# From the second pair of units on: three one-pass products of split operands in place of f32 products with Strassen

## The chip, the core and the metric

One NeuronCore of a Trainium2 chip. The metric is the device time of one execution, in microseconds (us), lower is better. Engine names: PE is TensorE, DVE is VectorE, ACT is ScalarE, POOL is GpSimd, SP is SyncE (it issues most DMAs).

## The reference

A Mamba-2 scan (4 batches, 8 heads, 768 tokens, 32 channels a head, state of 16) in chunks, then a feed-forward block with silu over 3072 tokens (256 to 2048 to 256). All in float32, but the two weight matrices come as float64.

```python
la = log(clip(a, 1e-6, 1)); cum = cumsum(la)          # per chunk
L = exp(cum[:, None] - cum[None, :]) * causal
y = ((C @ B.T) * L) @ x + (C @ state) * exp(cum)
state = exp(sum(la)) * state + (B * exp(cum[-1] - cum)).T @ x
x2 = y.transpose(0, 2, 1, 3).reshape(3072, 256)
h = x2 @ w_in
out = (h / (1 + exp(-h))) @ w_out
```

## The kernel before

**Units.** The 3072 tokens are 12 units of 256; two units make a pair (6 pairs), and three units a batch, whose state goes from unit to unit. For each unit the scan makes decays, a small score matrix and the state, and its result XM (256 channels by 256 tokens). Stage one multiplies XM by w_in and applies silu (result in gT); stage two multiplies by w_out; the result is transposed and stored.

**The scan of a unit.** `load_pa` and `load_ab` bring the decays `a`, spread over partitions by the DMA; f_P (L284 to L291) and f_E (L319 to L336) clamp them on VectorE and make prefix products with a scan instruction (L304 is E's). f_B (L341, POOL) makes BT from E; f_T (L347) or f_TP transposes B and C; f_T2 (L367) and f_C (L373) scale them; f_D0 (L391) and f_G0 (L406) are PE products into the PSUM tile gy; f_M (L417) multiplies the scores by E on VectorE; f_S (L432) carries the state, f_SM (L440) spreads it on ScalarE; f_Y (L460 and L469) makes y in gy, and f_X (L482) evacuates it to XM.

**Weights.** A weight piece (16 of them, `W`) is loaded raw as float64 words (L156). ScalarE (`w_size`, L164 and L168), VectorE (`w_bits`, L176 to L180) and POOL (L184) make f32 from it. Seven raw buffers; w_bits(n) issues the load of piece n+7.

**Stage one.** For units 0 to 3, f_s1 (L505): f32 products of 128x256, silu at L507. From pair 2 on, f_x1 does the two units of a pair with Strassen's seven products in place of eight (L703), with sums on VectorE (L706), copies and silu on ScalarE (L717, L709), and sums of weights and inputs made ahead (f_SW L675, f_XT L686).

**Stage two.** s2_pair, also with seven products in place of eight (L611 and L648, in the one-bank tile o_ps). Its operand sums are made by VectorE (f_T1 L544) and by accumulating DMAs of POOL (f_TS L553); partial results are copied by ScalarE (L588) and added by POOL (L558); f_out (L564, L566) transposes on VectorE and stores by SP. Stage two of a pair is laid piece by piece (`f_s2(n)`) between the products of the next pair's stage one.

**Order.** The instructions of each engine stand in the order in which the program text issues them (`manual_schedule`): the list `steps`, the loops over `j` and `scan_plan`. Each engine works in order, and waits are placed where tiles are shared. PSUM's eight banks are four of gy (one tile, `ps_s`), three of hp and one of o_ps.

**The start.** SP issues, in this order: a for the first batch (L192), C of unit 0 (L115), a again (L200), x of unit 0 (L122), three weight pieces (L156), B, C (L107) and x (L122) of unit 1, and more weight pieces. PE, while it waits, runs `busy` fillers (L226, L228). The decays of units 0 and 1 come by a small product (f_Ab, L312), those of later units by load_ab.

Of the kernel before, what the change touches and what calls it, by code (L numbers as in the profile page):

```python
# [9 lines left out]
U32 = mybir.dt.uint32  # L10
BF16 = mybir.dt.bfloat16
AF = mybir.ActivationFunctionType
# [9 lines left out]
def kernel(  # L22
# [36 lines left out]
    loads = ctx.enter_context(tc.tile_pool(name="loads", bufs=3))  # L59
    loads2 = ctx.enter_context(tc.tile_pool(name="loads2", bufs=2))  # L60
    rawp = ctx.enter_context(tc.tile_pool(name="rawp", bufs=7))
    wtp = ctx.enter_context(tc.tile_pool(name="wtp", bufs=3))
    sc = ctx.enter_context(tc.tile_pool(name="sc", bufs=1))
    sc2 = ctx.enter_context(tc.tile_pool(name="sc2", bufs=2))
    xmp = ctx.enter_context(tc.tile_pool(name="xmp", bufs=4))
    gpool = ctx.enter_context(tc.tile_pool(name="gpool", bufs=4))
    tpool = ctx.enter_context(tc.tile_pool(name="tpool", bufs=1))
    ppool = ctx.enter_context(tc.tile_pool(name="ppool", bufs=5))
    opool = ctx.enter_context(tc.tile_pool(name="opool", bufs=2))
# [5 lines left out]


    pa, ab, bn, tbc, xt = ({} for _ in range(5))
# [4 lines left out]
    def load_pa(u, q):  # L82

        b, t0 = at(u)
        pa[u] = loads.tile([128, UT], FP32, name="pa")
        q.dma_start(out=pa[u], in_=bass.AP(tensor=a.tensor, offset=a.offset + b * H * S + t0,
                                           ap=[[S, H], [0, N], [1, UT]]))

    def load_ab(u, q):

        b, t0 = at(u)
        ab[u] = loads2.tile([128, 2, H, Q], FP32, name="ab")
        for t in range(4):
            k, c = divmod(t, 2)
            q.dma_start(out=ab[u][64 * c:64 * c + 64, k],
                        in_=bass.AP(tensor=a.tensor, offset=a.offset + b * H * S + t0 + t * Q,
                                    ap=[[0, 64], [S, H], [1, Q]]))

    def load_n(u, i, q):

        b, t0 = at(u)
        if i == 0:
            t = bn[u] = loads.tile([128, 2, H, N], FP32, name="bn")
        else:
            t = tbc[u] = loads.tile([128, 2, 2, 8, N], FP32, name="tbc")[:, 0]
        for k in range(2):
            q.dma_start(out=t[:, k], in_=(B, C)[i][b, :, t0 + 128 * k:t0 + 128 * k + 128].rearrange("h p n -> p h n"))  # L107

    def load_t(u, i, q):

        b, t0 = at(u)
        if u not in tbc:
            tbc[u] = loads.tile([128, 2, 2, 8, N], FP32, name="tbc")
        for g in range(4):
            q.dma_start(out=tbc[u][32 * g:32 * g + 32, i],  # L115
                        in_=(B, C)[i][b, 2 * g:2 * g + 2, t0:t0 + UT].rearrange("e (t r) n -> t e r n", r=8))

    def load_x(u, q):
        b, t0 = at(u)
        xt[u] = loads.tile([128, 2, H, D], FP32, name="xt")  # L120
        for k in range(2):
            q.dma_start(out=xt[u][:, k], in_=x[b, :, t0 + 128 * k:t0 + 128 * k + 128].rearrange("h p d -> p h d"))  # L122

    def load_unit(u):
        load_pa(u, nc.sync)
        if 0 < u < UPB:
            load_n(u, 1, nc.sync)
        else:
            load_t(u, 0, nc.sync)
            load_t(u, 1, nc.sync)  # L130
        load_n(u, 0, nc.sync)
        load_ab(u, nc.sync)
        load_x(u, nc.sync)

    w_in_sb = const.tile([128, KC, d_ff], FP32, name="w_in_sb")
    w_out_sb = const.tile([128, NF, d_model], FP32, name="w_out_sb")
# [5 lines left out]
    raw, wu, wv = {}, {}, {}  # L142

    def w_piece(n):
        which, j = W[n]
        if which == "i":
            return wi[:, :, j * WF:(j + 1) * WF], w_in_sb[:, :, j * WF:(j + 1) * WF]
        return wo[:, 2 * j:2 * j + 2], w_out_sb[:, 2 * j:2 * j + 2]

    def load_w(n, q):  # L150
        src, dst = w_piece(n)
        if src.dtype == FP32:
            q.dma_start(out=dst, in_=src)
            return
# [3 lines left out]


    def w_size(n, what="uv"):  # L160
        if n in raw:
            if "u" in what:
                u = wu[n] = wtp.tile([128, 2, WF], FP32, name="wu")
                nc.scalar.activation(u, raw[n][:, :, :, 1].bitcast(FP32), AF.Abs)  # L164
            if "v" in what:
                v = wv[n] = wtp.tile([128, 2, WF], FP32, name="wv")

                nc.scalar.activation(v, raw[n][:, :, :, 0], AF.Copy, scale=2.0 ** -51, bias=2.0)  # L168

    def w_bits(n, parts=1):  # L170
        dst = w_piece(n)[1]
        if n in raw:
            u, v, hi = wu.pop(n), wv.pop(n).bitcast(U32), raw[n][:, :, :, 1]


# [3 lines left out]

# [7 lines left out]


    A0, A1 = 96, 96 + S // Q
    early = gpool.tile([128, NF, UT], FP32, name="gT")  # L190
    ach = early[:, 0:2].rearrange("p a (h t) -> p (a h) t", t=Q)
    nc.sync.dma_start(out=ach[A0:A1], in_=bass.AP(tensor=a.tensor, offset=a.offset, ap=[[Q, S // Q], [S, H], [1, Q]]))  # L192

    flat = early.rearrange("p f t -> p (f t)")
    QZ = 8 * (Q + 1)
    pa01 = flat[:, 6 * UT:8 * UT]
    pz01, one01, pfx01 = (flat[:, 8 * UT + QZ * i:8 * UT + QZ * (i + 1)] for i in range(3))
# [8 lines left out]
    load_x(1, nc.sync)  # L206

    mark = const.tile([1, RAW - 5], U32, name="mark")
    for n in range(3, RAW):
        if n > 4:  # L210
            nc.sync.dma_start(out=mark[:, n - 5:n - 4], in_=raw[n - 2][0:1, 0, 0, 0:1])
        load_w(n, nc.sync)


    def f_A():
        nc.vector.tensor_scalar(out=ach[A0:A1], in0=ach[A0:A1], scalar1=1.0, scalar2=1e-6, op0=ALU.min, op1=ALU.max)
        nc.vector.memset(ach[A0:A1, :, 0:1], 0.0)


    idle = early[:, 4].bitcast(BF16)  # L220
    nc.vector.memset(idle, 0.0)

    def busy(n, small=0):
# [3 lines left out]
        for i in range(small):  # L227
            nc.tensor.matmul(out=t[:64, :64], lhsT=idle[:, 0:64], rhs=idle[:, 64:128], start=True, stop=True)  # L228

    nc.vector.memset(ach[0:A0], 0.0)  # L230

    sel = early[:, 2:4].rearrange("p a (s c t) -> p (a s) c t", s=2, c=2)
    nc.gpsimd.memset(sel, 0.0)
    nc.gpsimd.affine_select(out=sel, in_=sel, pattern=[[-2, 4], [-1, 2], [0, 64]], compare_op=ALU.not_equal,
                            fill=1.0, base=-A0, channel_multiplier=1)

    diag1 = early[:, 5:6, 0:Q]
# [15 lines left out]

# [11 lines left out]

    pz = const.tile([128, 4, Q + 1], FP32, name="pz")
    one = const.tile([128, 4, Q + 1], FP32, name="one")
    for t, n in ((pz, 0.0), (one, 1.0)):
        nc.gpsimd.memset(t, 0.0)
        if n:  # L270
            nc.gpsimd.memset(t[:, :, 0:1], n)
    E, M, BT, BH, CT, CE, CW, PFX, ST, SM, DP, XM, GTS, BX = ({} for _ in range(14))
# [3 lines left out]

# [7 lines left out]
    def f_P0(u):  # L284
        nc.vector.tensor_scalar(out=pz[:, :, 1:], in0=pa.pop(u).rearrange("p (c t) -> p c t", t=Q),
                                scalar1=1.0, scalar2=1e-6, op0=ALU.min, op1=ALU.max)

    def f_P1(u):

        PFX[u] = sc2.tile([128, 4, Q + 1], FP32, name="pfx")  # L290
        nc.vector.tensor_tensor_scan(out=PFX[u].rearrange("p c t -> p (c t)"),  # L291
                                     data0=pz.rearrange("p c t -> p (c t)"),
# [3 lines left out]
    def f_P(u):  # L296
        f_P0(u)
        f_P1(u)

    def scan_E(u, g0, n, t):  # L300

        if g0 == 0:
            E[u] = sc.tile([128, 2, H, Q], FP32, name="E")
        nc.vector.tensor_tensor_scan(out=E[u].rearrange("p k h t -> p (k h t)")[:, Q * g0:Q * (g0 + n)],  # L304
                                     data0=t.rearrange("p g t -> p (g t)"),
                                     data1=diag[:, 0:n].rearrange("p g t -> p (g t)"),
                                     initial=0.0, op0=ALU.mult, op1=ALU.add)

    def f_Ab(u, k):

        ab[u, k] = t = ps_h.tile([128, H, Q], FP32, name="hp")
        nc.tensor.matmul(out=t.rearrange("p h t -> p (h t)"),  # L312
                         lhsT=sel[:A1, 2 * u + k].rearrange("r c m -> r (c m)"),
                         rhs=ach[:A1].rearrange("r h t -> r (h t)"), start=True, stop=True)

    def f_Ek(u, k):
        scan_E(u, H * k, H, ab.pop((u, k)))

    def f_E0(u, i, n):  # L319

        t = ab[u].rearrange("p k h t -> p (k h) t")[:, 2 * H // n * i:2 * H // n * (i + 1)]
        nc.vector.tensor_scalar(out=t, in0=t, scalar1=1.0, scalar2=1e-6, op0=ALU.min, op1=ALU.max)
        nc.vector.memset(t[:, :, 0:1], 0.0)  # L323

    def f_E1(u, i, n):

        g = 2 * H // n
        t = ab[u].rearrange("p k h t -> p (k h) t")[:, g * i:g * (i + 1)]
        scan_E(u, g * i, g, t)
        if i == n - 1:  # L330
            ab.pop(u)

    def f_E(u):
        f_E0(u, 0, 1)
        f_E1(u, 0, 2)
        f_E1(u, 1, 2)  # L336

    def f_B(u, engine=nc.gpsimd):

        BT[u] = sc.tile([128, 2, H, N], FP32, name="BT")  # L340
        engine.tensor_tensor(out=BT[u], in0=bn[u], in1=E[u][:, :, :, Q - 1:Q].to_broadcast([128, 2, H, N]),  # L341
# [3 lines left out]

# [6 lines left out]

# [10 lines left out]
    def f_T2(u, e):  # L363

        if e == 0:
            CE[u] = sc.tile([128, 2, UT], FP32, name="ce")
        nc.scalar.activation(CE[u][:, e], CT[u], AF.Copy, scale=par[:, e:e + 1])  # L367

    def f_C(u):

# [5 lines left out]
    def f_D0(u, early=False):  # L376

# [3 lines left out]
        n = 3 if last else 4  # L381
# [6 lines left out]
        for t in range(n):  # L388
# [8 lines left out]
    def f_G0(u):  # L397

        bh, ce = BH.pop(u), CE[u]
# [14 lines left out]
    def f_M(u, k):  # L414

        M[u] = m = E[u].rearrange("p k (g e) t -> p k g (e t)", e=2)
        nc.vector.tensor_tensor(out=m[:, k], in0=DP[u][:, :, 128 * k:128 * k + 128], in1=m[:, k], op=ALU.mult)  # L417

    def f_S(u, t0=0, t1=4):

        first, last = u % UPB == 0, u % UPB == UPB - 1
        if first and t0 == 0:
            ST[u] = sc2.tile([128, 4, 64], FP32, name="st")
        if not last and t1 == 4:
# [583 lines left out]
```

## Time and profile before

| what | value |
|---|---|
| median of 3 runs | 350.76 us (350.61 to 354.09) |
| profiled execution: span, first to last instruction | 348.7 us; its own time is not given apart |
| busy, of the span | PE 342.7 us, DVE 204.6, ACT 162.8, POOL 113.0 |
| granted PE clock | 1.00 in every window |
| DVE busy in 50 to 70 us | 19.64 of 20 |
| DMA moved | 42.66 MB, 122 GB/s |

Lines of the profile have the form: source line, engine, operation, output<-inputs, partitions x elements, count | busy us, mean ns of one | idle of the engine just before, and what ended it. PEld is the weight load of PE, which runs beside the products. Timeline lines begin with the start and the length in us; lines of the chain too. An f32 product of 128x128 by 128x256 stands as two records of two passes each. The mean of a product's record includes the flow through the array, so products overlap, and the pace is read from groups of them.

### The profile page before, as it was taken

The page shows a single profiled execution, that of the slowest core. Times are in us where ns is not written, and L with a number is a line of the kernel's source. Part 1 is how long each engine was busy: PE and PEld are TensorE (multiplying, and loading weights), DVE is VectorE, ACT ScalarE, POOL GpSimd, SP SyncE. Part 2 cuts the span into 40 slices and gives each one's busy share as a digit, 9 for nine tenths or more (in the row PEclk, how much of TensorE's full clock was granted, in tenths as well). Part 3 has the DMA queues.
Part 4 walks back from the last instruction along what each step waited for, and adds up shares of the span by engine and source line. Part 5 has one row for each costly group of instructions (what it writes and reads, how often), then busy time and mean ns, then how long its engine had stood idle before and what let it go on. Part 6 is the DMA issues. An engine that isn't in the chain of part 4 may idle for free.

```text
span 348.7 us, 8382 instructions
## 1 busy us (share of the span) xinstructions
PE 342.7 (98%) x3324; PEld 288.5 (83%) x3324; DVE 204.6 (59%) x406; ACT 162.8 (47%) x399; POOL 113.0 (32%) x140
## 2 busy tenths in 40 slices
PE   8999999999999999999999999999999999999996
PEld 3678888888888888888888888888888888888886
DVE  7998799976795664544663563564652241233912
ACT  3578395323323545455645454644545454454010
POOL 4355245444285032244042244042235112041200
DMA  6877997799857598948178965056604237512202
GB/s 130 203 237 174 241 313 126 132 199 218 144 102 126 124 186 149 169 102 138 21 159 163 187 112 90 16 98 125 115 2 75 39 60 144 107 24 53 41 7 46
DMA packets 117056, 42.66 MB, mean 122 GB/s; under 512 B 102424, under 2 KB 108824, under 8 KB 117016
## 3 DMA queue, kind: packets, MB, share of 16 engines
q1 hardware_dynamic: 110472, 25.73, 35.8%
q0 software_dynamic: 4464, 16.25, 25.0%
q8 instruction: 26, 0.43, 0.6%
q10 hardware_dynamic: 2080, 0.13, 0.4%
q14 instruction: 14, 0.11, 0.1%
HBM read 22.70 MB, written 3.15 MB: 74 GB/s over the span
## 4 chain that ended last, share of the span: by engine, by line
PE 96%; DVE 1%; issue 1%; POOL 1%; ACT 0%; DVEq 0%; POOLq 0%
PE o_ps L648 36%; PE hp L703 28%; PE hp L505 16%; PE hp L648 3%; PE gy L469 2%; PE gy L406 2%; PE o_ps L611 2%; PE gy L460 2%; PE gy L391 1%; PE hp L626 1%; PE hp L312 1%; PE o_ps L226 1%; POOL w_in_sb L184 1%; DVE E L417 0%; PE o_ps L228 0%
## 5 line engine op out<-in xcount | busy, mean ns | idle before, releaser
L706 DVE TENSOR_TENSOR gT<-hp,p 128x256 f32<-128x256 f32 x64 | 26.9, 420 | 73.6 <-ACT p L717 37.6
L648 PE MATMUL o_ps<-gT,w_out_sb 128*128 128x256 f32 x240 | 60.4, 379 | 0.0
L709 ACT ACTIVATE gT<-gT 128x256 f32<-128x256 f32 x96 | 39.7, 414 | 43.9 <-DVE gT L706 43.9
L505 PE MATMUL hp<-XM,w_in_sb 128*128 128x256 f32 x256 | 59.3, 381 | 0.9 <-ACT XM L482 0.5
L505 PEld LDWEIGHTS hp<-XM,w_in_sb 128*128 128x128 f32 x256 | 48.0, 190 | 8.7 <-POOL w_in_sb L184 1.4
L703 PE MATMUL hp<-raw 128*128 128x256 f32 x192 | 52.7, 380 | 0.0
L558 POOL TENSOR_TENSOR ps<-ps 128x256 f32<-128x256 f32 x35 | 29.6, 845 | 71.1 <-ACT ps L588 69.8
L648 PEld LDWEIGHTS o_ps<-gT,w_out_sb 128*128 128x128 f32 x240 | 45.4, 190 | 6.3
L553 POOL DMA_DIRECT2D gT<-gT x31 | 27.9, 929 | 65.7 <-DVE TN L544 21.5
L703 PEld LDWEIGHTS hp<-raw 128*128 128x128 f32 x192 | 36.2, 190 | 5.4 <-POOL ps L558 0.6
L717 ACT ACTIVATE p<-hp 128x256 f32<-128x256 f32 x64 | 24.6, 384 | 27.4 <-PE hp L703 25.9
L706 DVE TENSOR_TENSOR gT<-hp,u 128x256 f32<-128x256 f32 x32 | 13.6, 424 | 38.6 <-PE hp L703 38.6
L703 PE MATMUL hp<-XM,w_in_sb 128*128 128x256 f32 x128 | 34.1, 389 | 0.0
L507 ACT ACTIVATE gT<-hp 128x512 f32<-128x512 f32 x32 | 18.9, 595 | 26.4 <-PE hp L505 26.3
L703 PEld LDWEIGHTS hp<-XM,w_in_sb 128*128 128x128 f32 x128 | 23.3, 190 | 4.3 <-issue 1.0
L304 DVE TENSOR_TENSOR_SCAN E<-ab,diag 128x256 f32<-128x256 f32 (+1 forms) x32 | 25.1, 826 | 0.8 <-DVE ab L323 0.5
L341 POOL TENSOR_TENSOR BT<-bn,E 128x256 f32<-128x256 f32 x12 | 9.4, 780 | 47.5 <-DVE E L304 39.4
L648 PE MATMUL o_ps<-gT,wu 128*128 128x256 f32 x88 | 22.4, 380 | 0.0
L648 PE MATMUL o_ps<-gT,wv 128*128 128x256 f32 x88 | 22.2, 380 | 0.0
L648 PE MATMUL o_ps<-gT,raw 128*128 128x256 f32 x80 | 20.5, 380 | 0.0
L588 ACT ACTIVATE ps<-o_ps 128x256 f32<-128x256 f32 x35 | 13.3, 383 | 14.8 <-PE o_ps L648 13.0
L703 PE MATMUL hp<-raw,w_in_sb 128*128 128x256 f32 x64 | 19.1, 380 | 0.0
(126 smaller groups left out, 522.3 us busy)
## 6 DMA issues: line engine op xcount, KB each, us to landing
gT<-gT POOLq DMA_DIRECT2D x31, 512.0 KB, 6.3
ab<-in_a_dram SPq DMA_DIRECT2D x40, 128.0 KB, 3.1
raw<-in_moe_w_in_dram SPq DMA_DIRECT2D x8, 512.0 KB, 5.1
raw<-in_moe_w_out_dram SPq DMA_DIRECT2D x8, 512.0 KB, 6.5
xt<-in_x_dram SPq DMA_DIRECT2D x24, 128.0 KB, 5.1
out_dram<-ot SPq DMA_DIRECT2D x92, 32.0 KB, 2.6
bn<-in_B_dram SPq DMA_DIRECT2D x22, 64.0 KB, 5.3
tbc<-in_C_dram SPq DMA_DIRECT2D x40, 32.0 KB, 3.4
```

The costliest lines, as they stand in the source:

```text
L304: nc.vector.tensor_tensor_scan(out=E[u].rearrange("p k h t -> p (k h t)")[:, Q * g0:Q * (g0 + n)], data0=t.rearrange("p g t -> p (g t)"), ...
L341: engine.tensor_tensor(out=BT[u], in0=bn[u], in1=E[u][:, :, :, Q - 1:Q].to_broadcast([128, 2, H, N]), op=ALU.mult)
L505: nc.tensor.matmul(out=hp[:, i], lhsT=w_in_sb[:, kc, f * 128:(f + 1) * 128], rhs=xm[:, kc], start=(kc == 0), stop=(kc == KC - 1))
L507: nc.scalar.activation(GTS[g][:, :, j], hp, AF.Silu)
L553: nc.gpsimd.dma_start(out=o[:, js], in_=a[:, js], accum_op=ALU.add)
L558: engine.tensor_tensor(out=o, in0=p, in1=q, op=op)
L588: nc.scalar.activation(p[m].rearrange("p (k c t) -> p c k t", c=2, k=2), o.rearrange("p (c k t) -> p c k t", c=2, k=2), AF.Copy)
L648: nc.tensor.matmul(out=o, lhsT=w(j), rhs=g()[:, j], start=(j == 0), stop=(j == last))
L703: nc.tensor.matmul(out=o, lhsT=w, rhs=x_, start=start, stop=True, skip_group_check=True)
L706: nc.vector.tensor_tensor(out=o, in0=p, in1=q, op=ALU.add)
L709: nc.scalar.activation(o, i, AF.Silu)
L717: nc.scalar.activation(o, i, AF.Copy)
```

## The change

From pair 1 on, each operand of the two stages is split into parts that hold 12 bits: a high part h, a remainder l = x - h, and d = (1 + 2^-12) h - x. Three products, h of the one operand with h of the other, l with l and d with d, are made in the type float32r and accumulated in PSUM: a burst with h and l, then a scaling by 1 + 2^-12 on ScalarE, then d. The weights are split in the same way. So there are three products in place of one f32 product; Strassen's sums, both stages', are gone, and so are POOL's accumulating DMAs. Pair 0 stays f32, now without Strassen (f_s1, and f_n2 with products of 512 columns). Line numbers below are those of the changed kernel.

The main pieces of the new order (`...` where code is left out):

```python
def w_high(n):                                     # ACT, L200
    t = WK[n, "h"] = small([128, 2, WF], FR)
    nc.scalar.activation(t, WT[n], AF.Copy, scale=LESS * Z)
def w_rest(n, what="ld"):                          # DVE, L205: "r" in the lists
    ...
def f_XH(u): ...                                   # ACT, L466: h of a unit's y
def f_XL(u): ...                                   # DVE, L472, L473: its l and d
def epoch(G, e, fills=(0, 0)):                     # stage one of four blocks of 128
    t = ps_s.tile([128, 4, 512], FP32, name="gy")
    for p in range(2):
        for i in range(2 * p, 2 * p + 2):
            s1_mm(t[:, i], G, 4 * e + i, "hl", True)           # L553, 16 products in a row
        nc.scalar.activation(t[:, 2 * p:2 * p + 2], t[:, 2 * p:2 * p + 2], AF.Copy, scale=1.0 + Z)
    for p in range(2):
        f_s2(fills[p])                                         # L533, stage two
        for i in range(2 * p, 2 * p + 2):
            s1_mm(t[:, i], G, 4 * e + i, "d", False)
        g = GT[G, 2 * e + p] = large([128, 2, 512])
        nc.scalar.activation(g, t[:, 2 * p:2 * p + 2], AF.Silu, scale=BACK)
def f_h(G, i): ...                                 # ACT, L576, 128x1024
def f_ld(G, i):                                    # DVE, L581 and L582, 128x1024 each
    g, h = GT.pop((G, i)), HT.pop((G, i))
    l, d = large([128, 2, 512], FR), large([128, 2, 512], FR)
    ...
def f_ev(P, what): ...                             # ACT L540, DVE L544: end of a pair's stage two

def step(G, n):                                    # four steps a pair
    u = 2 * G + 2 + n // 2
    ...
    S2.extend(NEXT)
    f_s2(6)
    if prev: f_h(*prev[0])
    if more and n % 2 == 0: f_G(u); f_BX(u); f_M(u)            # in gy
    elif more: f_Y(u); f_YS(u)                                 # in gy
    if prev: f_h(*prev[1])
    f_s2(12)
    if G > 1 and n == 1: f_s2(24); f_ev(G - 1, "ad")
    epoch(G, n, (3, 3))                                        # in gy
    ...
    if G == 1: steps(early[n])                                 # weights: r, h
    if prev: f_ld(*prev[0])
    if more and n % 2 == 0: f_S(u); f_SM(u)
    elif u + 1 < NU and n % 2 == 1 and more: f_E(u + 1); f_B(u + 1)
    if prev: f_ld(*prev[1])
    ...
```

f_ld also puts 12 products of stage two into the list NEXT, which the next step takes up. Where the step ends in `...`, the transposes of unit u + 1, its prefix and cw, XH, XL, the loads and the output of a pair are issued. So gy (four banks) holds in turn a burst of the scan (D0 and G, or Y) and the four blocks of an epoch; accumulators of stage two hold the other four. All 4 KB tiles (`large`: silu results, h, l, d, outputs) come from one pool of 12 buffers taken in turn. After the last pair, 48 products of stage two remain, then f_ev and two f_out.

The decays of units 2 to 11 are now clamped once for all, at the start, on POOL, and go to DRAM (az, ac), from where load_ab and load_pz (eight DMAs a unit) spread them:

```diff
+    for b in range(batch):
+        nc.sync.dma_start(out=araw[CPB * b:CPB * b + CPB], ...)     # after load_x(1)
...
+    nc.gpsimd.memset(acp[:, :, 0:1], 0.0)
+    for t in (azt, acp[:, :, 1:]):
+        nc.gpsimd.tensor_scalar(out=t, in0=araw, scalar1=1.0, scalar2=1e-6, op0=ALU.min, op1=ALU.max)   # L285
+    nc.gpsimd.memset(azt[:, :, 0:1], 0.0)
+    nc.gpsimd.dma_start(out=az, in_=azt.rearrange("p h t -> p (h t)"))
+    nc.gpsimd.dma_start(out=ac, in_=acp.rearrange("p h t -> p (h t)"))
...
-    nc.vector.tensor_scalar(out=t, in0=t, scalar1=1.0, scalar2=1e-6, op0=ALU.min, op1=ALU.max)
-    nc.vector.memset(t[:, :, 0:1], 0.0)
+    nc.vector.tensor_tensor_scan(out=o, data0=src, data1=diag..., initial=0.0, op0=ALU.mult, op1=ALU.add)   # f_E, L319
```

These POOL instructions stand in the program before the first f_B. The order of POOL at the start is then: memsets and selects, L285 twice, a memset, two DMAs, BT of unit 0 (L324), cw (L352), the weight sums (L194). Between f_s1 of pair 0 and pair 1, f_n2 is interleaved with weight pieces 13 to 15, the remainders `r` and the scans of units 3 and 4:

```python
for n, todo in ((2, "b13 s14 2X"), (2, "r0 3T h2"), (2, "b14 s15 3E 3B"), (2, "3P 3C r1 h3"), (2, "b15 3GMS"),
                (2, "4L r2 h4"), (2, "r3 4T"), (2, "3Y h5"), (2, "4E 4B 4P 4C"), (2, "5L 3X h6 h7"), (2, "r4 r5 h8 h9")):
    f_n2(n); steps(todo)
early = {0: "r6 r7 h10 h11", 1: "r8 r9 h12 h13", 2: "r10 r11 h14 h15", 3: "r12 r13 r14 r15"}
```

## The prediction, on record before the run

> **What bounds the kernel now.** First the page: span, busy shares and the chain of work that ended last.
>
> ```profile
> span 348.7 us, 8382 instructions
> ...
> PE 342.7 (98%) x3324; PEld 288.5 (83%) x3324; DVE 204.6 (59%) x406; ACT 162.8 (47%) x399; POOL 113.0 (32%) x140
> ...
> PE 96%; DVE 1%; issue 1%; POOL 1%; ACT 0%; DVEq 0%; POOLq 0%
> ```
>
> TensorE is 98% busy and 96% of the chain: only its own work, or a new wait of it, can move the end. Next, the pace, in the chain told in order of time:
>
> ```profile
> 163.92 2.21 PE hp L703 x10
> ...
> 170.01 1.73 PE hp L703 x8
> ...
> 217.82 2.21 PE hp L703 x10
> ...
> 271.84 2.21 PE hp L703 x10
> ...
> 277.94 1.73 PE hp L703 x8
> ```
>
> Eight records are four f32 products of 256 columns: 1.73/8 = 0.216 us per record of two passes. One of the steady pairs recurs every 53.9 us (163.92, 217.82, 271.84). Then the start, POOL's timeline and SP's queue:
>
> ```profile
> 8.07 0.73 POOL L341 TENSOR_TENSOR BT<-bn,E 128x256 f32<-128x256 f32 x1 [2.75 <-DVE E L304]
> 9.98 0.68 POOL L373 TENSOR_TENSOR cw<-ct,gT 128x256 f32<-128x256 f32 x1 [1.18 <-DVE gT L280]
> 14.11 1.42 POOL L184 TENSOR_TENSOR w_in_sb<-wu,wv 128x256 uint32<-128x256 uint32 x2 [3.44 <-DVE wv L180]
> ```
>
> ```profile
> 9.34 5.18 SPq L107 DMA_DIRECT2D tbc<-in_C_dram  x2
> 14.57 1.31 SPq L122 DMA_DIRECT2D xt<-in_x_dram  x2
> 15.93 1.09 SPq L156 DMA_DIRECT2D raw<-in_moe_w_in_dram  x2
> ```
>
> POOL makes unit 0's BT at 8.07, and everything of the scan hangs on it; SP is still issuing unit 1's x at 15.88. Last, the rows by shape, for prices on VectorE and ScalarE:
>
> ```profile
> L417 DVE TENSOR_TENSOR E<-gy,E 128x512 f32<-128x512 f32 x24 | 15.4, 681 | 0.0
> ...
> L304 DVE TENSOR_TENSOR_SCAN E<-hp,diag 128x512 f32<-128x512 f32 x4 | 4.9, 1221 | 0.2
> ...
> L675 DVE TENSOR_TENSOR raw<-w_in_sb 128x1024 f32<-128x1024 f32 x2 | 2.5, 1270 | 0.0
> ...
> L675 DVE TENSOR_TENSOR raw<-w_in_sb,raw 128x1024 f32<-128x1024 f32 x1 | 1.2, 1218 | 0.0
> ```
>
> Successive VectorE instructions overlap by some 0.08 us (two of L417 take 1.28 together in the timeline), so I charge 0.6 for a two-input 128x512 and 1.15 for a 128x1024.
>
> **TensorE's own work.** From pair 1 on, each pair has 96 + 96 products of 512 columns. If a float32r product is one pass it costs 0.216, as any 512 column-passes do now, with the weight load (190 ns a row) hidden as now: 41.5 us a pair. Scans, by busy time of L469, L406, L460, L391 (10.3+8.3+7.9+5.4)/12 = 2.66 a unit, add 5.3: 46.8 instead of 53.9. No run here shows the dtype. Bounds: 0.216, and twice that if it needs two passes; the first is taken because f32's four passes already run at 512 columns per 0.216. Pair 0 stays f32 and loses Strassen: 32 products of 512 columns, 4x0.216 each, 27.6.
>
> The Trainium skill ("TensorE: Matmul & The Clock Gate", Back-to-back issue gap) puts a sustained stream of 512-column products at about 131 ns each. That would make the 960 products 82 us cheaper than 0.216 does; the rows show no stream that fast.
>
> Without any wait: stage one of pair 0 with unit 2's scan ends at 50.5 (start of L611 in the timeline); then 27.6 for stage two of pair 0, 8.0 for units 3 to 5, 31.1 for pair 1 (144 products): 117.2. Pairs 2, 3, 4: 140.4. Pair 5, with no scan: 41.5. The last 48 products, no longer laid under a later pair: 10.4. Then the end: two ScalarE copies and two VectorE additions 2.0, two 128x512 transposes 1.6 (L564 has 432 ns for half), four DMA issues and a landing of 2.6 (out_dram): 8. Sum 317.5. So the most that the change can gain is 31 us.
>
> **The new wait at the start.** POOL now clamps `araw` (L285, twice) and issues two DMAs (az, ac) ahead of BT of unit 0. The four araw loads stand behind unit 1's x in SP's queue: issue from 15.9 at 0.45 each, and in front of them x, whose median to landing is 5.1. Landing 20.3 (19.0 to 21.5). A POOL tensor_scalar of 512 elements is in no row: between memset 0.53 and the two-input 1.40; I take the one-input select, 0.67. DMA issues on POOL: L553 has 0.93 (0.45 if like SP's). BT starts at 20.3+1.3+0.2+1.9 = 23.7 and ends at 24.45; unit 0's L391 products, at 9.67 now, start at 24.5: +14.8 us (12.2 to 17.8). Behind the waiting POOL stand BT, cw and all weight sums; behind them the state update, M and the weight bits on VectorE, SM and w_size on ScalarE, Y and stage one on TensorE. Nothing covers it: az is wanted only for unit 2.
>
> The granted clock is 1.00 in every window, but the five fillers at 1.26 take 2.31 us, and three at 11.02 take 0.81. The same page (What's actually happening) says that an idle window of about 3.4 us drops the clock to half, and the same length of work raises it again. This idle of 15 us would by that rule cost up to 1.7 us more; I charge none, since VectorE's chain leads there.
>
> **VectorE's backlog before pair 2.** After the bits of weight piece 8 (36.4 now) VectorE still has pieces 9 to 15 at 2.36 each (49.08, 51.45, 53.81 in the timeline), scans of units 2 to 4, and the new remainders `r`, 32 at 0.6. What TensorE waits for, walked in program order: unit 3's E ends 28.5 after 36.4 (six pieces 14.2, two E 4.8, prefix, cw, M, state 3.2, XL, r0, transposes 3.5, hand-overs from ScalarE and TensorE 2.8), plus BT 0.8, so at 80.5 with the shift; TensorE is there at 50.5+14.8+8.6 = 73.9: 6.6. In step (1,1) SM sits on ScalarE behind the two evacuations of pair 0: 3.5; the burst behind ys: 1.2; M of unit 5 behind r8 to r11: 1.6; two SM and one M later: 1.3. Together 14.2 (bounds: 0, if VectorE is never late, and twice).
>
> **The steps of pairs 2 to 4.** Let T be the end of the burst of 16 products. TensorE ends the step at T+3.0 and reaches the next burst at T+8.0 (six products 1.3, D0 and G 1.1, twelve 2.6). In the last step of a pair the second remainder d0 gets its buffer (12 of 4 KB, in turn) only from the last three fills, T+1.75. From there VectorE: d0 1.15, E 2.4, l and d 2.3, prefix 0.7, XL 1.2, transpose 0.8, M 1.2 = 9.75, so M ends at T+11.6. D0 waits for BT 2.0, the burst for M 1.7. In the step after ev, the like chain costs 1.9; odd steps wait 0.6 each for SM, which ScalarE does behind the silu, and 0.3 for the second copy. A full pair: 7.0 of waits (bounds: 0 to 12), the first 3.9, as its d0 was free early: 17.9. ScalarE is loaded 16 of 25 us over two steps (128x1024 at 1.02: 384 for 256, 595 for 512, 211 more per 256). The 5 more loads a unit (22, not 17, by SP at 0.55) lie inside 25 us; were they late, E of a later unit would wait.
>
> What goes away, the accumulating DMAs, Strassen's sums and POOL's L558, lies beside TensorE now: credited at nothing.
>
> **Sum:** 317.5 + 14.8 + 14.2 + 17.9 = 364.4 of span, against 348.7. The median of the runs (350.76) is 2.1 over the profiled span; the profiled execution's own time is not given apart. Forecast 366.5.
>
> **Rivals.**
> Rival A, faster: VectorE keeps ahead. E, M and the remainders are done before TensorE arrives, no step waits: 317.5+14.8+2.1 = 334. For it: VectorE has 18.5 us of work in two steps of 23.4. Against: its order, d0 behind a late buffer and M behind XL. It decides where the chain from d0 to M is under 6.2 us instead of 9.75; already at 7.5, with half of the backlog gone, the time is under 347.
> Rival B, no change: the start is hidden (araw lands early or POOL's part is short), so 14.8 goes: 352. Against: POOL works in order, and SP issued x at 14.57 to 15.88.
> Rival C: further waits, weights and loads that arrive late behind the shift or hand-overs that I set at nothing: 385 and more. For it: my walk charges no semaphore latency.
> Rival D: float32r takes two passes: 960x0.216 = 207 more, about 570. This is the change not doing what it says.
>
> **Numbers.** Forecast 0.62, Rival A (and halfway to it) 0.18, Rival B 0.08, Rival C 0.08, Rival D 0.04. The measurement tells about 1% from no change: 347.3 to 354.3. Faster 0.18, same 0.10 (Rival B and a slice of the forecast's low end), slower 0.72. The range reaches from halfway into A, 343, over the bounds of the start (+3) and of the steps (+12) to 382; the forecast's own is 355 to 380.
>
> **What would show it.** Right: POOL idle to about 20 us, then L285, BT at about 24; TensorE idle from 10 to 24; L553 and L533 at 0.216 start to start; pair period about 54 with TensorE waiting for BT (L324) and M (L400) in even steps; VectorE the releaser in pairs 2 to 4; some 8 us from the last product to the end. Wrong: BT near 8; products at 0.43; a pair period of 47.

## The result, and the profile after

446.88 us median of 4 runs (445.94 to 448.55) against 350.69 for the kernel before: ratio 1.273, 95% interval 1.267 to 1.279. Slower, as forecast, but 80 us above the forecast of 366.5 and 65 above the upper end of its range (382). The profiled execution took 445.94, its span is 444.2.

The page of the changed kernel: span, busy shares, the chain of work that ended last, and the first group of part 5.

```profile
span 444.2 us, 7604 instructions
...
PE 352.3 (79%) x3082; PEld 246.4 (55%) x3082; DVE 250.5 (56%) x338; ACT 197.3 (44%) x293; POOL 50.5 (11%) x62
...
PE 65%; ACT 16%; DVE 8%; issue 4%; SPq 3%; POOL 1%; DMA 0%; DVEq 0%; ACTq 0%; POOLq 0%
...
L553 PE MATMUL gy<-xk,s2k 128*128 128x512 f32 x480 | 135.8, 419 | 53.8 <-ACT gy L562 36.6
```

TensorE fell from 98% to 79% of a longer span, and ScalarE, 0% of the chain before, is 16% of it: more than VectorE, which the prediction had watched. The waits of TensorE show what it waited for (us in total, times, longest):

```profile
PE gy L553 <- ACT gy L562: 36.6, 40, 1.4
PE gy L553 <- ACT r4k L568: 13.9, 20, 1.2
PE gy L368 <- POOL BT L324: 10.9, 3, 7.6
PE hp L368 <- POOL BT L324: 10.4, 1, 10.4
PE gy L434 <- issue: 5.8, 8, 2.4
PE gy L553 <- DVE ab L400: 2.5, 2, 1.3
```

50.5 us are waits of stage one for ScalarE's passes over gy: 40 for the scaling copy (two in each of 20 epochs), 20 for silu. One epoch in the timeline:

```profile
239.02 2.11 PE L553 MATMUL gy<-xk,s2k 128*128 128x512 f32 x8 [1.26 <-DVE ab L400]
...
241.21 1.01 ACT L562 ACTIVATE gy<-gy 128x1024 f32<-128x1024 f32 x1 [4.95 <-DVE r4k L582]
...
242.27 2.12 PE L553 MATMUL gy<-xk,s2k 128*128 128x512 f32 x8 [1.15 <-ACT gy L562]
...
244.49 1.01 ACT L562 ACTIVATE gy<-gy 128x1024 f32<-128x1024 f32 x1 [2.27 <-PE gy L553]
245.55 0.77 PEld L553 LDWEIGHTS gy<-xk,s2k 128*128 128x128 f32 x4 [0.90 <-ACT gy L562]
245.55 1.20 PE L553 MATMUL gy<-xk,s2k 128*128 128x512 f32 x4 [0.46 <-ACT gy L562]
...
246.85 1.03 ACT L568 ACTIVATE r4k<-gy 128x1024 f32<-128x1024 f32 x1 [1.35 <-PE gy L553]
...
247.93 1.20 PE L553 MATMUL gy<-xk,s2k 128*128 128x512 f32 x4 [0.47 <-ACT r4k L568]
```

The burst of 16 products that the prediction let run in one piece is cut in two. The second eight write banks 2 and 3 of gy; the copy at 241.21 works on banks 0 and 1; still they start 0.05 us after the copy's end. The four d products at 247.93 wait in the same way for silu over the other half. Products and passes take turns: a pair recurs every 67.1 us (the first bursts of pairs 2 and 3 start at 171.88 and 239.02), not 53.8.

The start, on POOL, went nearly as worked out: BT (L324) at 21.80 against 23.7.

```profile
18.77 0.60 POOL L285 TENSOR_SCALAR s2k<-s2k 48x512 f32<-48x512 f32 x1 [13.69 <-DMA s2k<-in_a_dram]
19.46 0.61 POOL L285 TENSOR_SCALAR r4k<-s2k 48x512 f32<-48x512 f32 x1
20.12 0.10 POOL L286 MEMSET s2k<- 48x8 f32 x1
20.53 0.74 POOL L287 DMA_DIRECT2D az<-s2k  x1 [0.30 <-POOL s2k L286]
21.27 0.52 POOL L288 DMA_DIRECT2D ac<-r4k  x1
21.80 0.65 POOL L324 TENSOR_TENSOR BT<-s2k,ab 128x256 f32<-128x256 f32 x1
```

### The profile page after: what moved, and what is told of

It is laid out like the page before. It is cut to its first block, busy times and chain, and to the rows that moved or that the text cites. A ratio compares the mean times of both kernels' runs of the same rounds, so it can differ in the third digit from the quotient of the medians.

```text
span 444.2 us, 7604 instructions
## 1 busy us (share of the span) xinstructions
PE 352.3 (79%) x3082; PEld 246.4 (55%) x3082; DVE 250.5 (56%) x338; ACT 197.3 (44%) x293; POOL 50.5 (11%) x62
## 4 chain that ended last, share of the span: by engine, by line
PE 65%; ACT 16%; DVE 8%; issue 4%; SPq 3%; POOL 1%; DMA 0%; DVEq 0%; ACTq 0%; POOLq 0%
PE gy L553 29%; PE hp L533 17%; ACT gy L562 9%; PE hp L484 5%; PE hp L513 5%; ACT r4k L568 4%; PE o_ps L533 3%; PE gy L443 2%; DVE ab L319 2%; PE gy L434 2%; PE gy L382 1%; SPq L123 1%; DVE ab L400 1%; DVE r4k L582 1%; DVE xk L473 1%
## 5 line engine op out<-in xcount | busy, mean ns | idle before, releaser
L553 PE MATMUL gy<-xk,s2k 128*128 128x512 f32 x480 | 135.8, 419 | 53.8 <-ACT gy L562 36.6
L553 PEld LDWEIGHTS gy<-xk,s2k 128*128 128x128 f32 x480 | 87.6, 193 | 97.7 <-ACT gy L562 53.9
L533 PE MATMUL hp<-r4k,s2k 128*128 128x512 f32 x400 | 110.3, 401 | 0.0
L581 DVE TENSOR_TENSOR r4k<-r4k 128x1024 fp32r<-128x1024 f32 x40 | 48.6, 1215 | 72.3 <-PE hp L533 41.4
L562 ACT ACTIVATE gy<-gy 128x1024 f32<-128x1024 f32 x40 | 40.3, 1008 | 107.7 <-PE gy L553 97.9
L533 PEld LDWEIGHTS hp<-r4k,s2k 128*128 128x128 f32 x400 | 75.8, 192 | 18.4 <-issue 1.2
L582 DVE SCALAR_TENSOR_TENSOR r4k<-r4k 128x1024 fp32r<-128x1024 f32 x40 | 51.4, 1286 | 41.0 <-PE hp L533 41.0
L568 ACT ACTIVATE r4k<-gy 128x1024 f32<-128x1024 f32 x40 | 41.0, 1026 | 55.2 <-PE gy L553 55.2
L576 ACT ACTIVATE r4k<-r4k 128x1024 fp32r<-128x1024 f32 x40 | 41.7, 1052 | 0.7 <-PE hp L533 0.7
L324 POOL TENSOR_TENSOR BT<-bn,ab 128x256 f32<-128x256 f32 x10 | 12.0, 1205 | 220.6 <-DVE ab L319 187.3
L533 PE MATMUL o_ps<-r4k,s2k 128*128 128x512 f32 x80 | 31.2, 390 | 0.0
L513 PE MATMUL hp<-r4k,s2k 128*128 128x512 f32 x64 | 30.3, 626 | 0.0
L194 POOL TENSOR_TENSOR s2k<-s2k 128x512 uint32<-128x512 uint32 (+1 forms) x20 | 23.4, 1179 | 32.1 <-DVE s2k L190 32.1
L484 PEld LDWEIGHTS hp<-r4k,s2k 128*128 128x128 f32 x128 | 23.8, 190 | 4.7 <-issue 1.1
L205 DVE SCALAR_TENSOR_TENSOR s2k<-s2k 128x512 fp32r<-128x512 f32 x32 | 20.7, 706 | 0.0
L513 PEld LDWEIGHTS hp<-r4k,s2k 128*128 128x128 f32 x64 | 12.5, 200 | 14.7 <-issue 14.2
L421 ACT ACTIVATE sm<-st,par 128x128 f32<-128x128 f32 (+1 forms) x24 | 8.0, 383 | 21.7 <-DVE st L414 21.7
```

What stands on the lines that cost most here:

```text
L194: nc.gpsimd.tensor_tensor(out=dst[:, :, fs].bitcast(U32), in0=u[:, :, fs], in1=v[:, :, fs], op=ALU.add)
L205: nc.vector.scalar_tensor_tensor(out=t, in0=f32(WK[n, "h"]), scalar=-BACK if p == "l" else -(BACK + 1.0), in1=WT[n], op0=ALU.mult, op1=ALU ...
L484: nc.tensor.matmul(out=hp[:, i], lhsT=WT[j][:, kc, 128 * i:128 * i + 128], rhs=XM[:, 2 * kc:2 * kc + 2, u], start=(kc == 0), stop=(kc == K ...
L513: nc.tensor.matmul(out=NP["o"][m], lhsT=WT[8 + f // 2][:, f % 2, 128 * m:128 * m + 128], rhs=G0[f // 2][:, f % 2], start=(f == 0), stop=(f ...
L533: nc.tensor.matmul(out=ACC[P, 2 * (p == "d") + m], lhsT=WK[8 + f // 2, p][:, f % 2, 128 * m:128 * m + 128], rhs=rhs, start=(f == 0 and p ! ...
L553: nc.tensor.matmul(out=o, lhsT=WK[j, q][:, kc, 128 * i:128 * i + 128], rhs=xs[:, 2 * kc:2 * kc + 2], start=(start and q == "h" and kc == 0 ...
```

## The experiments

**Two tiles (e1).**

```diff
-    ps_s = ctx.enter_context(tc.tile_pool(name="ps_s", bufs=1, space=bass.MemoryType.PSUM))
+    ps_s = ctx.enter_context(tc.tile_pool(name="ps_s", bufs=2, space=bass.MemoryType.PSUM))
...
-        t = ps_s.tile([128, 4, 512], FP32, name="gy")
+        t = [ps_s.tile([128, 2, 512], FP32, name="gy", tag="gy") for _ in range(2)]
...
-            s1_mm(t[:, i], G, 4 * e + i, "hl", True)
+            s1_mm(t[p][:, i % 2], G, 4 * e + i, "hl", True)
-        nc.scalar.activation(t[:, 2 * p:2 * p + 2], t[:, 2 * p:2 * p + 2], AF.Copy, scale=1.0 + Z)
+        nc.scalar.activation(t[p], t[p], AF.Copy, scale=1.0 + Z)
```

> Edit: the four banks of gy become two tiles of two banks each (the same four banks, the same work; M and the copy of Y are split in two because each half now lies in another tile). Theory S (the whole tile gy is one thing for the waits, so that TensorE's second burst, its d products and the next d products each wait for ScalarE's pass over the other half): the waits of L553 for the copy (36.6 us) and for silu (13.9 us) all but go, each with the 0.16 us that a product flows on and the hand-overs, about 3 us in each of 20 epochs; the pair period falls from 67 to 52 to 56 us and the time from 447 to 380 to 395 us. Rival theory V (VectorE's chain of remainders, E and M sets the period, and the waits for ScalarE only fill time that TensorE would spend waiting for VectorE): the period stays over 62 us and the time over 420 us, with TensorE waiting for BT and M instead.

Measured: 383.93 us (381.30 to 384.85), 1.094 of before (1.089 to 1.098), 63 us less. TensorE's waits, and a burst in one piece over ScalarE's copy:

```profile
PE gy L371 <- POOL BT L327: 13.8, 4, 7.5
PE hp L371 <- POOL BT L327: 10.7, 1, 10.7
PE gy L439 <- issue: 6.2, 8, 2.3
PE o_ps L245 <- DVE s2k L240: 1.3, 1, 1.3
PE gy L560 <- ACT gy L569: 1.2, 6, 0.2
```

```profile
199.00 3.90 PE L560 MATMUL gy<-xk,s2k 128*128 128x512 f32 x16
...
201.12 1.01 ACT L569 ACTIVATE gy<-gy 128x1024 f32<-128x1024 f32 x1 [2.71 <-PE gy L560]
...
202.73 0.85 PE L540 MATMUL hp<-r4k,s2k 128*128 128x512 f32 x3
...
202.99 1.01 ACT L569 ACTIVATE gy<-gy 128x1024 f32<-128x1024 f32 x1 [0.86 <-PE gy L560]
```

The same banks, the same passes: 50.5 us of waits became 1.2. TensorE's busy time fell too, from 352.3 to 338.0, over the same products: eight in a row count 2.11, sixteen 3.90, so each cut of a burst adds some 0.3. An epoch, from its first product to the end of its d products and the products between them, takes 7.0 us here (199.00 to 205.99) and 9.9 in the changed kernel (239.02 to 248.96). The pair recurs every 55.6 us (159.69, 215.33). Theory S holds, theory V falls.

**Clamps later (e2), and both (e3).**

```diff
     nc.gpsimd.memset(acp[:, :, 0:1], 0.0)
-    for t in (azt, acp[:, :, 1:]):
-        nc.gpsimd.tensor_scalar(out=t, in0=araw, ...)
-    nc.gpsimd.memset(azt[:, :, 0:1], 0.0)
-    nc.gpsimd.dma_start(out=az, in_=azt.rearrange("p h t -> p (h t)"))
-    nc.gpsimd.dma_start(out=ac, in_=acp.rearrange("p h t -> p (h t)"))
...
     w_bits(1, 2)
+    for t in (azt, acp[:, :, 1:]):
+        nc.gpsimd.tensor_scalar(out=t, in0=araw, ...)
+    nc.gpsimd.memset(azt[:, :, 0:1], 0.0)
+    nc.gpsimd.dma_start(out=az, in_=azt.rearrange("p h t -> p (h t)"))
+    nc.gpsimd.dma_start(out=ac, in_=acp.rearrange("p h t -> p (h t)"))
     load_unit(2)
```

> Edit: POOL's two clamps, the memset and the DMAs of az and ac stand behind the weight sums of pieces 0 and 1 instead of ahead of BT of unit 0. Start theory: BT of unit 0 is made near 8 instead of 21.7 us, the first products of L368 start near 9.7 instead of 22.5, stage one of pair 0 moves up by 12 to 15 us, and the time falls by 10 to 15 us, to 432 to 437. Rival: weights and VectorE's bits are late anyhow, the time moves by under 4 us.

> Both edits, two tiles and the later clamp. If the two losses are apart from each other: the sum, 367 to 382 us. If VectorE's backlog takes over once TensorE no longer waits for ScalarE and starts early: 390 us and more, with the waits of TensorE for BT (POOL, behind E) before pair 1 grown to over 15 us.

Measured: e2 439.23 us (1.254 of before, 1.250 to 1.259), 7.7 less than the changed kernel; e3 374.34 (1.067, 1.065 to 1.069), 9.6 less than e1. The two losses add up. Less came back than the 10 to 15 expected, and more than the rival's 4. The wait moved: in e2 TensorE waits 2.6 us for BT of unit 1, which now stands behind the clamps, and stage two of pair 0 starts at 57.18, against 65.25 changed and 50.54 before.

**Half the columns (e4).**

```diff
-                    NEXT.append(partial(s2_mm, G, 2 * i + k, m, p, t[:, k]))
+                    NEXT.append(partial(s2_mm, G, 2 * i + k, m, p, t[:, k, 0:256]))
```

> Leaves out work: stage two from pair 1 on takes 256 of the 512 columns of each product (the same number of products and of weight loads); half of those outputs are not computed. Load theory (the pace of 0.227 us of a float32r product is set by the weight load of 0.19 us that comes with each, and a hand-over): six products of L533 still take about 1.36 us, start to start. Stream theory (512 columns through the array set it): six take 0.8 to 1.2 us, down to what six loads take.

Six products from start to start, first in the changed kernel, then here:

```profile
253.54 0.39 PE L533 MATMUL o_ps<-r4k,s2k 128*128 128x512 f32 x1
253.76 1.30 PE L533 MATMUL hp<-r4k,s2k 128*128 128x512 f32 x5
254.90 0.39 PE L533 MATMUL o_ps<-r4k,s2k 128*128 128x512 f32 x1
255.12 1.30 PE L533 MATMUL hp<-r4k,s2k 128*128 128x512 f32 x5
```

```profile
251.42 0.28 PE L533 MATMUL o_ps<-r4k,s2k 128*128 128x256 f32 x1
251.53 0.76 PE L533 MATMUL hp<-r4k,s2k 128*128 128x256 f32 x5
252.13 0.28 PE L533 MATMUL o_ps<-r4k,s2k 128*128 128x256 f32 x1
252.25 0.76 PE L533 MATMUL hp<-r4k,s2k 128*128 128x256 f32 x5
```

1.36 us for six of 512 columns, 0.227 each; 0.72 for six of 256, 0.12 each, below even the 0.8 to 1.2 of the stream theory. Columns set the pace, not the weight load, which takes 0.19 in both and so runs beside the products. (The one run, which leaves those outputs out, took 424.54.)

**108 rows (e5).** In the run with both edits TensorE is at half pace long after the start; with zeros in 96 more rows of the decays' product it is not.

```diff
-    ach = small([CPB, H, Q])
+    ach = small([128, H, Q])              # a in rows 96 to 107, zeros in 0 to 95
...
-        nc.tensor.matmul(out=..., lhsT=sel[:, 2 * u + k]..., rhs=ach...)
+        nc.tensor.matmul(out=..., lhsT=sel[:A1, 2 * u + k]..., rhs=ach[:A1]...)
```

Two transposes and one decay product (two records), in e3 and then in e5:

```profile
7.31 0.69 PE L335 MATMUL o_ps<-ident,s2k 128*128 128x128 f32 x2
...
12.86 2.07 PE L308 MATMUL hp<-s2k 12*128 12x512 f32 x2
```

```profile
5.83 0.38 PE L337 MATMUL o_ps<-ident,s2k 128*128 128x128 f32 x2
...
9.63 1.12 PE L310 MATMUL hp<-s2k 108*128 108x512 f32 x2
```

> Edit, on top of two tiles and the later clamp: the small product that spreads the decays of units 0 and 1 (L310 of the changed kernel) takes 108 rows again, with zeros in the first 96, as the kernel before has it, in place of 12. In the run with both edits TensorE runs at half pace from its first product to about 27 us, though the granted clock shows 1.00 there; in the kernel before the half pace ends at 6.5 us. Row theory (products that fill 12 of 128 rows do not bring the array up to pace): the pace is full from about 7 us, stage one of pair 0 starts 4 to 7 us earlier, the time falls from 374.3 to 367 to 371 us. Rival (the half pace comes from the idle stretches and the rows do not matter): the pace stays half to 25 us and the time within 1 us of 374.3.

Measured: 372.82 us (1.062 of before, 1.058 to 1.066). The pace came as the row theory said; the time, 1.5 less, came as neither said. Stage one of pair 0 starts 6.5 us earlier (14.79 against 21.31), but only 1.5 of it reach the end: BT of unit 1 still waits for the clamps (3.7, with a halved clock behind it), and later TensorE waits for unit 3 anyway.

**Order of the steps (e6), and before pair 2 (e7).**

```diff
             f_M(u)
+            f_S(u)
...
+        if more and n % 2 == 0:
+            f_SM(u)
         f_s2(12)
...
-        elif u + 1 < NU and n % 2 == 1 and more:
+        if more and n % 2 == 0 and u + 1 < NU:
             f_E(u + 1)
             f_B(u + 1)
```

> On top of that, the order of the steady steps: E and BT of the next unit in the even step, between nothing but its two pairs of remainders, instead of the odd step behind the late d0; the state update right behind M, and SM ahead of the epoch's passes on ScalarE. Chain theory (of the 55 us of a pair some 6 are TensorE's waits for BT, M and SM, as the prediction had it): waits for BT fall from 2.4 to under 0.5 us a pair, SM's 0.4 twice a pair go, the pair period falls from 55 to 50 to 52 us, and the time by 8 to 14 us. Rival (d0's late buffer moves the wait to M and the remainders): the period stays over 54 and the time moves by under 4 us.

```diff
-    for n, todo in ((2, "b13 s14 2X"), (2, "r0 3T h2"), (2, "b14 s15 3E 3B"), (2, "3P 3C r1 h3"), (2, "b15 3GMS"),
-                    (2, "4L r2 h4"), (2, "r3 4T"), (2, "3Y h5"), ..., (2, "r4 r5 h8 h9")):
+    for n, todo in ((2, "3E 3B b13 s14 2X"), (2, "r0 3T h2"), (2, "b14 s15"), (2, "3P 3C h3"), (2, "b15 3GMS"),
+                    (2, "4L r1 h4"), (2, "4T"), (2, "3Y h5"), ..., (2, "h8 h9")):
```

> On top of that, between the first pair's stages: E and BT of unit 3 ahead of the bits of weight pieces 13 to 15, and the remainders r1 to r5 of the weights later (r2 to r5 in the first step of the second pair). Backlog theory (TensorE waits 7.5 us for unit 3's E behind weight work, and its clock halves after that): the wait for BT of unit 3 goes, the first product of the second pair starts 8 to 12 us earlier, the time falls by 6 to 12 us. Rival (VectorE has the same work in all, so the wait moves to M, Y or the first remainders): under 3 us.

Measured: e6 362.70 us (1.034, 1.030 to 1.038), 10.1 less than e5, as the chain theory said; the pair recurs every 51.2 us (213.86, 265.06) and no wait for BT or SM is left in pairs 2 to 4. e7 361.68 (1.030, 1.025 to 1.035), 1.0 less: its rival was right. The wait of 7.5 for BT of unit 3 became 3.6 for the scaled C of the same unit, whose transposes then stood behind remainders; the other two lines stood in e6 as well (4.4 each):

```profile
PE gy L557 <- ACT ys L464: 4.4, 2, 2.3
PE hp L368 <- POOL BT L324: 4.0, 1, 4.0
PE gy L382 <- ACT ce L347: 3.6, 1, 3.6
```

**Towards a version that beats both (e8 to e12).** First e8, on top of e6, with the order of `todo` in place of e7's, and the clamps of e2 between f_B(1) and `load_unit(2)`:

```diff
-    def load_unit(u, what="abpnx"):
+    def load_unit(u, what="anbxp"):
...
+    for n, todo in ((2, "3E 3B b13 s14"), (2, "3T h2"), (2, "b14 s15"), (2, "3P 3C h3"), (2, "3GMS b15"),
+                    (2, "4L 2X h4"), (2, "4T r0"), (2, "3Y h5"), ..., (2, "r1 h8 h9")):
```

> On top of the steps' order: the clamps on POOL go behind BT of unit 1 (in the run with full rows they still stand ahead of it and TensorE waits 3.7 us for it, with a halved clock behind that); before the second pair, E, BT, the transposes and the prefix of unit 3 go ahead of the remainders of y and weights, M ahead of weight piece 15, and a unit's B is loaded ahead of its eight prefix loads. Theory (waits that were moved by the earlier edits, not removed: 4 us at the start, 3.6 to 7.5 before unit 3): TensorE has no wait over 1.5 us between 12 and 100 us, and the time falls from 362 to 350 to 356 us. Rival (VectorE has no room before 95 us, so another of its products is late): over 359 us.

Measured: 357.14 us (1.016, 1.009 to 1.023), between theory and rival: waits of 4.4 for the copy of Y (two), 2.6 for the scaled C and 2.3 for BT remain.

```diff
             scan(u + 1, "T")
+        if G == 1 and n % 2 == 0:
+            steps(early[n])               # was ahead of the remainders of silu
...
-    S2.extend(NEXT)
-    f_s2(48)
-    f_ev(G, "ad")
+    S2.extend(parts[0][:18] + parts[1][:6] + parts[0][18:] + parts[1][6:])   # by half of the outputs
+    f_s2(30)
+    f_ev(G, "ad", (0,))
```

> On top of that, the remainders of the weights behind the transposes in the even steps of the second pair (TensorE waits twice 2.2 us there for the copy of Y, which stands on ScalarE behind the scaled C, which waits for the transposes), and at the end the 48 products sorted so that one half of the outputs is added up and stored beside the last 18 products. Theory: another 3 to 6 us, 345 to 352 us, at or just under the kernel before. Rival: the two waits come back as waits for remainders and the end is set by the second half alone: under 1.5 us.

Measured: 368.27 us (1.047, 1.041 to 1.053), 11.1 more than e8. Each edit brought a long wait of TensorE:

```profile
PE hp L537 <- DVE s2k L205: 6.2, 1, 6.2
PE gy L368 <- POOL BT L324: 4.3, 2, 2.4
PE hp L537 <- DVE r4k L588: 3.6, 2, 3.2
```

Remainders of w_out (L205) came after the products that need them. At the end the wait of 3.2 is for a remainder of a silu result (L588); in the timeline that remainder itself waited 2.5 us for a store of outputs, and the next one 2.5 for sorted products, which held 4 KB buffers. Why the store came so late for it is not shown.

```diff
+            f_T(u + 1, 0)                 # e10, even steps, right behind f_SM(u)
+            f_T(u + 1, 1)
...
-    S2.extend(NEXT)                       # e11
-    f_s2(48)
+    S2.extend(NEXT[:24] + sorted(NEXT[24:], key=lambda q: q.args[2]))
+    f_s2(36)
+    f_ev(G, "ad", (0,))
+    f_out(G, 0)
+    f_s2(12)
```

> On top of the run with start and unit 3 (the two further edits of the last run are dropped: it showed TensorE waiting 6.2 us for remainders of the weights put too late, and 3.2 us at the end for a remainder of y whose buffer the sorted products held). In the even steps the transposes of the next unit go right behind the state update, ahead of all remainders; before the second pair, the transposes of unit 3 ahead of weight piece 13, and E, BT and the transposes of unit 4 two steps earlier. Theory: the waits of TensorE for the copy of Y (2 x 2.2 us), for the scaled C of unit 3 (2.6) and for BT of unit 4 (1.6) go, and the time falls from 357 to 347 to 351 us. Rival (VectorE's work there is the limit, not its order): over 354 us.

> On top of that, only the last 24 products are sorted by half of the outputs, so that no buffer is held longer; the first half is added up, transposed and stored beside the last 12 products (2.7 us). Theory: the stretch from the last product to the end, 8.5 us, loses the first half's additions, transpose and half of the DMA issues: 1.5 to 3 us less than the run before it. Rival: the stores' landing sets the end, under 0.7 us.

Measured: e10 356.39 us (1.015, 1.012 to 1.018), 0.8 less than e8, so the rival was right: there are new waits for M (2.8) and x (1.4). e11 353.27 (1.007, 1.004 to 1.010), 3.1 less; the stretch from the last product to the end went from 8.6 us to 6.5, which is 2.1 of it.

```diff
-    def load_unit(u, what="anbxp"):
+    def load_unit(u, what="xanbp"):
...
-    (0, 5, "2PE 2B s9"), (1, 5, "2C b9 s10")
+    (0, 5, "2E 2B s9"), (1, 5, "2PC b9 s10")
...
-    early = {0: "r2 r3 r4 r5 h10 h11", 1: "r6 r7 r8 r9 h12 h13", 2: "r10 r11 h14 h15", ...}
+    early = {0: "r2 r3 r4 r5", 1: "r6 r7 r8 r9 h10 h11", 2: "r10 r11 h12 h13", ...}
```

> On top of the run with halves at the end: a unit's x is loaded first (TensorE waits 2.7 us for x of unit 3, and its clock is half in the next 5 us), E and BT of unit 2 go ahead of its prefix (VectorE idles 7.0 us there for the prefix loads), and in the second pair's first steps the scaling of weight pieces and of the first silu result on ScalarE goes behind the copy of Y (TensorE waits 2.3 us for it). Theory: these waits and the halved clock go, 353.3 falls to 345 to 349 us, under the kernel before (350.8). Rival (each moved load or pass is late somewhere else): over 351 us.

Measured: 360.01 us (1.028, 1.026 to 1.030), the rival. TensorE's named waits went (the copy of Y 0.3, x none), and others came: 5.1 for a remainder of a silu result (L587), 2.6 for B and 1.7 for SM. No version beat the kernel before; e11 comes within 0.7% of it, with TensorE busy 331.0 of 351.3 us.

## Why the prediction was wrong

The step that failed is the first sentence on the steps: with T the end of "the burst of 16 products", "TensorE ends the step at T+3.0". It let ScalarE's copy of one half of gy run beside products into the other half, and charged 0.3 for the second copy. In its place stands a wait per tile: whatever touches gy waits for the last pass over any part of gy. The epochs shown take 9.9 us and, with two tiles, 7.0; at 2.9 each, 20 epochs make 59. With the tile cut in two, 63 us went (e1), four fifths of the 80 that the forecast missed.

The other terms, as worked out and as measured:

| term | predicted | measured |
|---|---|---|
| shift of pair 0's stage two by the start | 14.8 | 14.7 (65.25 - 50.54) |
| TensorE's wait for BT of unit 3 | 6.6 | 7.6 |
| waits of a pair of 2 to 4 for BT, M, SM | 7.0 | 3.6 in pair 3 of the changed kernel (1.65, 1.26, 0.35, 0.32); with two tiles 2.4 for BT and 0.8 for SM |
| period of a pair of 2 to 4 | 53.8 | 67.1; 55.6 with two tiles |
| one float32r product of 512 columns | 0.216 | 0.227, so 960 x 0.011, some 10 more |
| last product to the end | 8 | 8.6 (435.6 to 444.2) |

364.4 + 62.6 (the spans of the changed kernel and e1, 444.2 - 381.6) + 10 = 437 of the 444.2. The waits behind the start, 14.2 and 17.9 in the sum, came to 21.7 with two tiles (13.8 for BT, 6.2 for SM, 1.7 for ScalarE's copies), 10 less, so some 17 are left that are not taken apart. Some of it is the clock: after the wait of 7.6 the granted clock is 0.61 from 82 to 88 us, and 12 records of L513 take 7.04 where 0.43 each would be 5.2.

Of the start the size was right and the mechanism incomplete. POOL's wait was there as described. The half pace behind it, which the prediction set at nothing, was on the path: from the first products behind BT to stage one of pair 0 it took 7.9 us (22.50 to 30.37), against 5.4 before (9.67 to 15.04). BT came 1.9 earlier than worked out; that the two errors about cancelled is luck. The granted clock falls to 0.75 from 14 to 16 us, after the last filler's end at 12.08, and is 0.50 from 16 to 28, though work resumes at 22.50. The Trainium skill ("TensorE: Matmul & The Clock Gate", What's actually happening) has the clock halved after an idle window of some 3.4 us and whole again after as much work. The fall of the granted clock agrees; its rise took longer here. But that the idle time caused the half pace is not shown at this place: two transposes took 0.69 at 7.31, ahead of the wait, and in e1 products are as slow behind the same wait while the granted clock reads 1.00. The wait for unit 3 shows it better: 20 records of L513 take 8.85 us ahead of it, 12 take 7.04 behind it.

That undoing POOL's order alone gave 7.7 fits a wait that moved to the next thing on its queue: BT of unit 1.

Rival C (385 and more, by hand-overs that the walk set at nothing) is where the time fell, with another mechanism and 62 more. Rivals A, B and D did not occur; two passes would have shown as 0.43.

E6 shows the chain theory of the steps right: with E, the state update and SM moved, the pair falls from 55.0 to 51.2, and the waits for BT and SM go (55.0 is e3's: 151.65 to 206.62; in e5, on which e6 stands, it is 55.6, 148.91 to 204.49, part of it at half pace). And it suggests why the change has little to win: 51.2 against 53.9 is 2.7 us a pair, about 11 over four pairs, against a pair 0 without Strassen, the 48 products and 8 us at the end, and the remainders that fill VectorE before pair 2.

## What to carry to other kernels

Where an engine works in place on half of a tile while another is to fill the other half, look in the built order for what the second one waits for: a tile is one thing for the waits here, and two tiles over the same banks cost 2.8 us of VectorE's busy time (250.5 to 253.3) and saved 63. A sum of busy times and of the waits one thinks of leaves out the others; walk one whole step product by product, hand-over by hand-over, through every engine that touches the accumulator. And a wait taken away is a gain only as far as the next late thing: in e2 the first products behind BT came 10.3 us earlier (12.16 against 22.50), and 7.7 reached the end.

## What the runs showed of the hardware

With 12 of 128 rows filled in the first four product records, TensorE was at half pace at 7.2 to 7.3 us in all five runs (0.69 for two transposes, the changed kernel and e1 to e4); with 108 rows it was at full pace by 7.0 in every other run (0.38 or 0.39). With 12 rows it rose near 12.5 us in e2 (L305 1.20 for two records) and not before 25 in e3, whose start differs by little, so the rule is not settled. The profile's granted clock says 1.00 all through e3's slow stretch: half pace has to be read from the length of known products there.

A wait of 2.4 us can be enough to halve the pace, and need not be. TensorE waits 2.40 us for BT in each of two pairs of e1, e3 and e5. Behind three of the six waits (both of e1, one of e5) the products go at half pace, behind the other three at full pace. In the first pair, e1 and then e3:

```profile
209.93 0.43 PE L371 MATMUL gy<-xt,BT 64*32 64x64 f32 x24 [2.40 <-POOL BT L327]
...
211.03 2.50 PE L540 MATMUL hp<-r4k,s2k 128*128 128x512 f32 x5
```

```profile
201.90 0.43 PE L366 MATMUL gy<-xt,BT 64*32 64x64 f32 x24 [2.40 <-POOL BT L322]
...
202.88 1.43 PE L535 MATMUL hp<-r4k,s2k 128*128 128x512 f32 x5
```

A float32r product is one record, an f32 product two. A float32r record of 512 columns takes 0.227 and one of 256 takes 0.12; an f32 record takes 0.43 and 0.216 (L513 in the changed kernel, L703 in the one before). So float32r needs half the time of an f32 record and some 11 ns more, and about a quarter of the time of an f32 product. The Trainium skill ("TensorE: Matmul & The Clock Gate", Back-to-back issue gap) puts a sustained stream at about 131 ns for 512 columns; no stream here came near it, so the measured 0.227 decides.
